# Low parts of keys and queries moved to VectorE, in a linear-attention and MLP kernel

## The chip, the core and the metric

The kernel runs on one core of a Trainium2 chip, as one program. The metric is the device time of one execution in microseconds (us), the median of several runs.

## The reference

Three layers follow each other on 4 batches of 576 tokens with 512 channels (8 heads of 64).

```python
def phi(x):                                  # x = q or k, times 64**-0.25
    h = einsum('bhsd,md->bhsm', x, omega) - sum(x*x, -1, keepdims=True)/2
    return exp(h - max(h, -1)) / sqrt(128)
kv  = einsum('bhsm,bhsd->bhmd', phi(k), v);  z = sum(phi(k), axis=2)
x   = einsum('bhsm,bhmd->bhsd', phi(q), kv) / (einsum('bhsm,bhm->bhs', phi(q), z) + 1e-6)
h   = relu(x.T @ w_tok1) @ w_tok2            # token mixing, 576 -> 256 -> 576
u   = x + h.T;   x = u + relu(u @ w_ch1) @ w_ch2           # channels, 512 -> 1536 -> 512
u   = x + real(fft(fft(x, axis=1), axis=2))
out = u + relu(layernorm(u) @ w_ff1) @ w_ff2               # 512 -> 2048 -> 512
```

The inputs of the MLP weights come as 64-bit words on the host side; the kernel turns ("widens") them into two 32-bit parts on the chip.

## The kernel before

Every matmul operand that matters for precision is split into a high part (rounded to fp32r) and a low part (the rest), and a product takes three matmuls: high by high, high by low, low by high.

**Attention.** The tokens stand in 18 tiles of 128. For each tile of keys or queries and each group g of 4 heads there is one *slot*. There are 72 slots, in this order: slots 0 to 9 are the keys of tiles k0 to k4 (two slots a tile); from slot 10 to 61 keys and queries alternate (k5 g0, q0 g0, k5 g1, q0 g1, k6 g0, ...); slots 62 to 71 are queries alone. In the loop of `attention()` the pass for slot n issues, engine by engine in program order (each engine runs its own instructions in that order):

- `load`: a tile of keys or queries is loaded by SP's queue six slots ahead of its first use (L385), with the values v (L390). The pool holds 4 such tiles, and 6 of v.
- `project`: six matmuls for slot n (L413) into a PSUM bank of tag A, of which there are four.
- `sums`: `kv_add` for the key slot n-3 (L447). A tile that holds the end of one batch and the start of the next (tiles 4 and 13) has a second, late part, one slot later.
- `queries`: for the query slot n-3, four transposes (L466) and ScalarE's copy into qpT (L474; for tiles 4 and 13 two half copies with zeros written by GpSimd beside them, L471, L472); for slot n-7 the transposed result goes to x2.
- `split_in`: four slots ahead of its first slot a tile is split. The high part is ScalarE's copy (L400; VectorE's for k1 and k3, L398), the low part t - h is one 128x512 subtraction on GpSimd (L401; on VectorE for k0 alone). Both parts are made in the same slot.
- `feature`: VectorE's maximum over each head (L427), then ScalarE's four exponentials (L431), or VectorE's subtraction and one exponential (L434, L435).
- `results`: for the query slot n-5 `numer` (L484, one PSUM pair N), and after g = 1 VectorE's `divide` (L493 to L507) and the split of the result, whose low part xl is GpSimd's (L514).
- `side.step(budget)`: a budget of VectorE time per slot for widening.
- from slot 36 on one piece of token mixing of a finished batch (L572 to L588), whose low part h1l is VectorE's (L576).

**Widening.** A chunk (4 chunks of 640 or 576 words for the token weights, then 28 slabs of 1024) is loaded (L264), worked in seven VectorE instructions (`take`, `rest`, `size`, `high`, `low`, `unit`, `scaled`: L275, L286, L290, L294, L298, L302, L306; planned at 0.68, 0.68, 0.69, 1.21, 1.21, 0.69 and 1.22 us for 1024 words, and in proportion for less) with one of ScalarE between (L282), and stored (L541 to L549, or L337). The class `Side` holds these pieces in a list, each with a planned VectorE time. A step adds its budget to a credit (at most 4.0) and issues pieces as long as the credit pays. Loads and stores cost nothing in it; a deferred one is issued four steps later. Before the change the budget is 0.7 us in slots 0 to 9, 0.4 in slots 10 to 35, and 1.2 from slot 36.

```python
            if n >= 0:
                side.step(SLOT0_US if n < 10 else SLOT1_US if n < 36 else SLOT_US)
```

By this plan, before the change, the loads of the first two chunks, and the first `take` behind them, stand in slot 0, and the store of the last token weights in slot 36.

After the attention come the two MLPs with the Fourier layer between them (L694, L816, L1129), in blocks of 512 tokens; widening goes on beside them.

Of the kernel before, what the change touches and what calls it, by code (L numbers as in the profile page):

```python
# [9 lines left out]
F32 = mybir.dt.float32  # L10
# [4 lines left out]
ALU = mybir.AluOpType  # L15
# [17 lines left out]

SLOT0_US, SLOT1_US, SLOT_US, FIRST_US, SHORT_US, CH_US, FF_US, SAVED_US = 0.7, 0.4, 1.2, 3.9, 1.2, 3.7, 3.7, 4.0


LAG, LAG_NUM, LAG_X, AHEAD_LOAD, AHEAD_SPLIT, DEFER = 3, 5, 7, 6, 4, 4
# [135 lines left out]
def pieces(t0, n):  # L175

    done = 0
    while done < n:
        b, s = divmod(t0 + done, S)
        step = min(n - done, S - s)  # L180
        yield done, step, b, s
        done += step
# [54 lines left out]
def mix_kernel(ctx: ExitStack, tc: tile.TileContext, qt, kt, va, om, w1, w2, wch, wff, t1, t2, out):  # L237
    nc = tc.nc
    pe, act, dve, pool, sync = nc.tensor, nc.scalar, nc.vector, nc.gpsimd, nc.sync
# [113 lines left out]
    def bank(tag):  # L353
        if tag not in pools:
            tag = "A"
        if tag == "A" and spare:

            tag = spare.pop(0)
            spare.append(tag)
        pl, bufs = pools[tag]  # L360
        return pl.tile([128, 512], F32, tag=tag, name=tag, bufs=bufs)
# [6 lines left out]
    e0 = p0.enter_context(tc.tile_pool(name="e0", bufs=3, side="right"))  # L368
    pl = ExitStack()
    ld = pl.enter_context(tc.tile_pool(name="ld", bufs=3))  # L370

    om_sb = e0.tile([128, 4, M], F32, tag="df", name="om_sb", bufs=2).rearrange("p a b -> p (a b)")[:, 0:256]
# [1 line left out]
    om_l = e0.tile([128, 256], F32R, name="om_l", bufs=1)  # L374

    def projection():
        sync.dma_start(out=om_sb, in_=om)
        act.mul(out=om_h, in_=om_sb, mul=scale)
        dve.scalar_tensor_tensor(out=om_l, in0=om_sb, scalar=scale, in1=om_h, op0=ALU.mult, op1=ALU.subtract)

    src = {}

    def load(kind, i):
        t = ld.tile([128, 4, 128], F32, tag="x", name=kind + "s", bufs=4)
        sync.dma_start(out=t, in_=(kt if kind == "k" else qt)[:, i])  # L385
        src[kind, i] = t
        if kind == "k":
            for part, row in enumerate([i] + [NT + c for c, j in enumerate(SPLIT) if j == i]):
                t = ld.tile([128, H, D + 1], F32, tag="v", name="v", bufs=6)
                sync.dma_start(out=t.rearrange("p h d -> p (h d)"), in_=va[row])  # L390
                src["v", i, part] = t

    def split_in(kind, i):
        t = src.pop((kind, i))
        h = ld.tile([128, 4, 128], F32R, tag="h", name=kind + "h")
        l = ld.tile([128, 4, 128], F32R, tag="l", name=kind + "l")
        if kind == "k" and i in (1, 3):
            dve.tensor_copy(out=h, in_=t)  # L398
        else:
            act.copy(out=h, in_=t)  # L400
        (dve if (kind, i) == ("k", 0) else pool).tensor_tensor(out=l, in0=t, in1=h, op=ALU.subtract)  # L401
        src[kind, i] = (h, l)

    proj = {}
    ft = {}
# [35 lines left out]
    def kv_add(i, g, part):  # L441

        off, n, b, s = part
        if s == 0:
            kvp[b, g] = bank("H")
        for hh in range(4):
            pe.matmul(out=kvp[b, g][:, hh * 65:hh * 65 + 65], lhsT=ft["k", i, g][:, hh, :],  # L447
                      rhs=src["v", i, int(off > 0)][:, 4 * g + hh, :], start=(s == 0 and hh == 0), stop=(s + n == S),
                      skip_group_check=True)
        if s + n == S:  # L450
            t = e0.tile([128, 4, D + 1], F32, tag=f"kvs{g}", name="kvs", bufs=2)
            act.copy(out=t.rearrange("p h d -> p (h d)"), in_=kvp[b, g][:, 0:260])
            kvs[b, g] = t
            if (b, g) == (B - 1, 1):
                spare.extend("AAH")
# [3 lines left out]
    num = {}  # L459
    xhl = {}  # L460

    def turn(i, g):
        tp = bank("S")
        f = ft.pop(("q", i, g))
        for hh in range(4):
            pe.transpose(tp[:, hh * 128:hh * 128 + 128], f[:, hh, :], ident)  # L466
        qpt[i, g] = []
        for off, n, b, _ in pieces(i * 128, 128):
            t = e0.tile([128, 4, 128], F32, tag="qpT", name="qpT", bufs=4)
            if n < 128:  # L470
                pool.memset(t[:, :, 64 - off:128 - off], 0.0)  # L471
                act.copy(out=t[:, :, off:off + n], in_=tp.rearrange("p (a b) -> p a b", a=4)[:, :, off:off + n])  # L472
            else:
                act.copy(out=t.rearrange("p a b -> p (a b)"), in_=tp)  # L474
            qpt[i, g].append((b, t))

# [10 lines left out]
    def divide(i):  # L487

        nm = num.pop(i)
        xt[i] = x = e0.tile([128, DM + 2], F32, tag="x", name="x", bufs=2)  # L490
        rd = e0.tile([128, 2, 4], F32, tag="rd", name="rd")
        n4 = nm[:, :, 0:260].rearrange("p g (h e) -> p g h e", e=65)
        dve.tensor_scalar(out=rd, in0=n4[:, :, :, 64], scalar1=float(M * 1e-6), scalar2=None, op0=ALU.add)  # L493
        dve.reciprocal(out=rd, in_=rd)

        def quarter(g, a, lo):
            dve.tensor_tensor(out=x[:, lo:lo + 128].rearrange("p (h e) -> p h e", e=64),  # L497
                              in0=n4[:, g, 2 * a:2 * a + 2, 0:64],
                              in1=rd[:, g, 2 * a:2 * a + 2].unsqueeze(2).to_broadcast([128, 2, 64]), op=ALU.mult)

        quarter(1, 0, 256)
        quarter(1, 1, 385)
        quarter(0, 0, 0)
        quarter(0, 1, 129)
        dve.tensor_tensor(out=x[:, 128:385:256], in0=nm[:, 1, 0:259:258], in1=rd[:, 1, 0:4:3], op=ALU.mult)  # L507
# [9 lines left out]
    def turn_x(i):  # L517
        x = xt.pop(i)
        tp = bank("S")
        for c in range(4):  # L520
            pe.transpose(tp[:, c * 128:c * 128 + 128], x[:, c * 128:c * 128 + 128], ident)
        t4 = tp.rearrange("p (c t) -> p c t", c=4)
        for off, n, b, s in pieces(i * 128, 128):
            if s == 0:
                x2[b] = xp.tile([128, 4, S], F32, tag="x2", name="x2")
            act.copy(out=x2[b][:, :, s:s + n], in_=t4[:, :, off:off + n])
# [66 lines left out]
    def last_tile(b):  # L593
        return ((b + 1) * S - 1) // 128
# [3 lines left out]
    for b in range(B):  # L598
# [3 lines left out]
        a = [("q", i, g) for i in range(qn, qe) for g in range(2)]  # L602
# [8 lines left out]
    side = Side()  # L611
# [87 lines left out]
    def attention():  # L699
        tiles = [(kind, i) for kind, i, g in order if g == 0]  # L700
        at = {t: order.index(t + (0,)) for t in tiles}
        late = {}
        n_all = len(order)

        def at_slot(n, kind):
            return order[n][1:] if 0 <= n < n_all and order[n][0] == kind else None

        def sums(n):
            if (t := at_slot(n - LAG, "k")) is not None:
                parts = list(pieces(t[0] * 128, 128))  # L710
                kv_add(*t, parts[0])
                if len(parts) > 1:
                    late[n + 1] = lambda: kv_add(*t, parts[1])
            if n in late:
                late.pop(n)()

        def queries(n):
            if (t := at_slot(n - LAG, "q")) is not None:
                turn(*t)
            t = at_slot(n - LAG_X, "q")  # L720
            if t is not None and t[1] == 1:
                turn_x(t[0])
                for b in range(B):
                    if t[0] == last_tile(b):
                        fill.extend(tok_mix(b))

        def results(n):
            if (t := at_slot(n - LAG_NUM, "q")) is not None:
                numer(*t)
                if t[1] == 1:  # L730
                    divide(t[0])
                    split_x(t[0])

        loads, splits = list(tiles), list(tiles)
        for n in range(-1, n_all + LAG_X):
            while loads and at[loads[0]] <= n + AHEAD_LOAD:
                load(*loads.pop(0))
            if n == n_all:
                enter_mlp()
            if 0 <= n < n_all:  # L740
                project(*order[n])
            sums(n)
            queries(n)
            while splits and at[splits[0]] <= n + AHEAD_SPLIT:
                split_in(*splits.pop(0))
            if 0 <= n < n_all:
                feature(*order[n])
            results(n)
            if n >= 0:
                side.step(SLOT0_US if n < 10 else SLOT1_US if n < 36 else SLOT_US)  # L750
            if fill and (len(fill) > 3 or n % 2 == 0):
                fill.pop(0)()
            for fn in early[:3]:
                fn()
            del early[:3]
# [434 lines left out]
```

## Time and profile before

| | |
|---|---|
| time, median of 3 runs | 970.43 us (970.21 to 976.52) |
| the profiled execution's own time | 972.31 us |
| its span (first to last instruction) | 970.2 us |
| PE busy | 949.7 us (98%) |
| VectorE (DVE) busy | 548.6 us (57%) |
| ScalarE (ACT) busy | 277.6 us (29%) |
| GpSimd (POOL) busy | 111.5 us (11%) |
| mean granted TensorE clock | 0.991 |

PE is TensorE's matmuls and PEld its weight loads. Matmuls overlap in the pipeline, so a PE shown as busy is not a PE at its peak: the distance from one start to the next tells its pace. Times in the rows count from the first instruction.

### The profile page before, as it was taken

How to read it: one execution, taken by the hardware profiler on the slowest of the kernel's cores; microseconds unless marked ns; L12 is line 12 of the kernel's file. 1: busy time of each engine (PE TensorE's matmuls, PEld its weight loads, DVE VectorE, ACT ScalarE, POOL GpSimd, SP SyncE). 2: the span in 40 equal slices, each digit the busy share in tenths (PEclk: the TensorE clock that was granted, in tenths of full speed). 3: DMA queues.
4: the chain of work that ended last, by engine and by line, in shares of the span. 5: the costliest groups of instructions: out<-in, count | busy, mean ns of one | idle time of the engine just before them, and what ended most of it. 6: DMA issues, size and time to landing. Idle time of an engine off the chain costs nothing.

```text
span 970.2 us, 13164 instructions
## 1 busy us (share of the span) xinstructions
PE 949.7 (98%) x5248; PEld 828.7 (85%) x5248; DVE 548.6 (57%) x1056; ACT 277.6 (29%) x621; POOL 111.5 (11%) x108
## 2 busy tenths in 40 slices
PE   7999999899999999999999999999999999999998
PEld 6999989888889988888888888888888888888897
DVE  5786988887776677766766442164346434411211
ACT  4786667642212222211311210111112111110111
POOL 2354334312110011000000000000000000000000
PEclk8899999999999999999999999999999999999999
DMA  7754554279899395364365952034103410251080
GB/s 260 241 194 161 183 184 161 104 271 334 336 351 406 126 370 207 136 251 177 116 210 208 378 174 86 1 130 174 44 1 124 162 62 1 99 205 44 16 324 30
DMA packets 33261, 170.80 MB, mean 176 GB/s; under 512 B 3632, under 2 KB 4272, under 8 KB 15664
## 3 DMA queue, kind: packets, MB, share of 16 engines
q1 hardware_dynamic: 27296, 126.91, 36.6%
q0 software_dynamic: 5904, 43.06, 11.6%
q8 instruction: 41, 0.67, 0.3%
q14 instruction: 20, 0.16, 0.1%
HBM read 132.08 MB, written 34.08 MB: 171 GB/s over the span
## 4 chain that ended last, share of the span: by engine, by line
PE 89%; DVE 7%; ACT 1%; issue 1%; DMA 1%; SPq 0%; DVEq 0%; ACTq 0%
PE H L694 35%; PE A L1129 20%; PE A L816 15%; PE A L413 3%; PE H L447 2%; PE N L484 2%; PE A L572 2%; PE S L994 1%; DVE mx L427 1%; DVE x L497 1%; PE S L1007 1%; DVE cvo L298 1%; PE S L585 1%; PE S L1113 1%; PE A L466 1%
## 5 line engine op out<-in xcount | busy, mean ns | idle before, releaser
L694 PE MATMUL H<-uh,w 128*128 128x512 f32 (+1 forms) x1120 | 341.0, 371 | 0.0
L694 PEld LDWEIGHTS H<-uh,w 128*128 128x128 f32 x1120 | 205.0, 189 | 34.9
L777 DVE SCALAR_TENSOR_TENSOR hl<-H,hh 128x512 fp32r<-128x512 f32 (+1 forms) x140 | 89.1, 637 | 256.3 <-ACT hh L776 256.1
L776 ACT ACTIVATE hh<-H 128x512 fp32r<-128x512 f32 (+1 forms) x140 | 77.8, 556 | 507.1 <-PE H L694 504.8
L694 PE MATMUL H<-ul,w 128*128 128x512 f32 (+1 forms) x560 | 206.3, 368 | 0.0
L1129 PE MATMUL A<-w,hh 128*128 128x512 f32 x576 | 146.8, 391 | 0.0
L1129 PEld LDWEIGHTS A<-w,hh 128*128 128x128 f32 x576 | 106.6, 188 | 21.0
L694 PEld LDWEIGHTS H<-ul,w 128*128 128x128 f32 x560 | 105.6, 189 | 16.8
L816 PE MATMUL A<-hh,w 128*128 128x512 f32 (+1 forms) x480 | 108.7, 369 | 0.0
L816 PEld LDWEIGHTS A<-hh,w 128*128 128x128 f32 x480 | 84.2, 188 | 15.0
L1129 PE MATMUL A<-w,hl 128*128 128x512 f32 x288 | 80.6, 390 | 0.0
L1129 PEld LDWEIGHTS A<-w,hl 128*128 128x128 f32 x288 | 54.1, 188 | 11.4
L431 ACT ACTIVATE f<-A,mx 128x128 f32<-128x128 f32 x204 | 58.9, 382 | 14.1 <-DVE mx L427 13.8
L816 PE MATMUL A<-hl,w 128*128 128x512 f32 (+1 forms) x240 | 59.2, 368 | 0.0
L427 DVE TENSOR_REDUCE mx<-A 128x4 f32<-128x512 f32 x71 | 48.4, 682 | 11.4 <-PE A L413 9.8
L816 PEld LDWEIGHTS A<-hl,w 128*128 128x128 f32 x240 | 42.6, 188 | 7.6
L447 PE MATMUL H<-v,f 128*128 128x65 f32 x320 | 44.4, 287 | 1.9 <-ACT f L431 1.3
L447 PEld LDWEIGHTS H<-v,f 128*128 128x128 f32 x320 | 43.2, 209 | 2.6 <-ACT f L431 1.8
L484 PE MATMUL N<-kvs,qpT 128*128 128x65 f32 x320 | 40.1, 270 | 3.0 <-DVE x L507 3.0
L484 PEld LDWEIGHTS N<-kvs,qpT 128*128 128x128 f32 x320 | 38.9, 193 | 3.7 <-POOL ql L401 2.4
L306 DVE SCALAR_TENSOR_TENSOR cvo<-cvo,cvy 128x1024 fp32r<-128x1024 f32 (+2 forms) x32 | 40.0, 1248 | 0.0
L294 DVE SCALAR_TENSOR_TENSOR cvo<-cvy,cvo 128x1024 int32<-128x1024 int32 (+2 forms) x32 | 38.9, 1215 | 0.5
(185 smaller groups left out, 1183.2 us busy)
## 6 DMA issues: line engine op xcount, KB each, us to landing
w<-kept SPq DMA_DIRECT2D x80, 1024.0 KB, 5.1
kept<-cvo POOLq DMA_DIRECT2D x21, 1024.0 KB, 6.8
stg<-in_wff_dram POOLq DMA_DIRECT2D x16, 1024.0 KB, 6.3
stg<-in_wch_dram SPq DMA_DIRECT2D x9, 1024.0 KB, 4.8
kept<-cvo SPq DMA_DIRECT2D x7, 1024.0 KB, 4.6
v<-in_va_dram SPq DMA_DIRECT2D x20, 260.0 KB, 3.8
ks<-in_kt_dram SPq DMA_DIRECT2D x18, 256.0 KB, 3.7
qs<-in_qt_dram SPq DMA_DIRECT2D x18, 256.0 KB, 4.0
```

The lines of the kernel that those rows point to most:

```text
L294: dve.scalar_tensor_tensor(out=st["h"], in0=st["y"].bitcast(I32), scalar=-0x80000000, in1=st["h"], op0=ALU.bitwise_and, op1=ALU.bitwise_or)
L306: dve.scalar_tensor_tensor(out=st["o"][:, 1, 0:n], in0=st["l"].bitcast(F32), scalar=2.0 ** -52, in1=st["y"], op0=ALU.mult, op1=ALU.mult)
L413: pe.matmul(out=pj[:, p_ * 256:p_ * 256 + 256], lhsT=a[:, c, :], rhs=w, start=(n == 0), stop=(n == 2), skip_group_check=True)
L427: dve.tensor_reduce(out=mx, in_=p4, axis=AX.X, op=ALU.max, negate=True)
L431: act.activation(out=f[:, hh], in_=p4[:, hh], func=AF.Exp, bias=mx[:, hh])
L447: pe.matmul(out=kvp[b, g][:, hh * 65:hh * 65 + 65], lhsT=ft["k", i, g][:, hh, :], rhs=src["v", i, int(off > 0)][:, 4 * g + hh, :], start=( ...
L484: pe.matmul(out=nm[:, hh * 65:hh * 65 + 65], lhsT=t[:, hh, :], rhs=kvs[b, g][:, hh, :], start=(c == 0), stop=(c == len(ts) - 1), skip_grou ...
L694: pe.matmul(out=hb[:, 0:n], lhsT=a[:, kk * 128:kk * 128 + 128], rhs=u[:, kk, 0:n], start=(c == 0), stop=(c == 11))
L776: act.activation(out=hh, in_=hb[:, 0:n], func=AF.Relu)
L777: dve.scalar_tensor_tensor(out=hl, in0=hb[:, 0:n], scalar=0.0, in1=hh, op0=ALU.max, op1=ALU.subtract)
L816: pe.matmul(out=acc[i][:, 0:cols], lhsT=a[:, cs], rhs=v, start=(j == 0 and c_ == 0), stop=(j == NCH - 1 and c_ == 2))
L1129: pe.matmul(out=acc[t], lhsT=a[:, t * 128:t * 128 + 128], rhs=w, start=(j == 0 and c_ == 0), stop=(j == NFF - 1 and c_ == 2))
```

## The change

- The low part of each tile of keys and queries goes from GpSimd to VectorE, and is issued one slot after the high part, ahead of that slot's splits and maximum (k0's at once, as before).
- Widening: no step before slot 2, steps with a budget of zero in slots 2 to 5 (they issue the first loads alone), 1.2 us in slots 6 to 9, 0.45 in 10 to 35, 1.2 from 36. By the planner the first `take` comes in slot 6, and the store of the last token weights in slot 38.
- The late part of `kv_add` comes two slots after the first instead of one, and first in its slot.
- The zeros beside half tiles of queries are written once, at the start, into one tile for each g.
- omega is loaded on ScalarE's queue instead of SP's.
- Three tiles of keys and queries in the pool instead of four, three whole qpT instead of four, two rd instead of three.

```diff
-SLOT0_US, SLOT1_US, SLOT_US, ... = 0.7, 0.4, 1.2, ...
+SLOT0_US, SLOT1_US, SLOT_US, ... = 1.2, 0.45, 1.2, ...
...
-        sync.dma_start(out=om_sb, in_=om)
+        act.dma_start(out=om_sb, in_=om)
...
-        t = ld.tile([128, 4, 128], F32, tag="x", name=kind + "s", bufs=4)
+        t = ld.tile([128, 4, 128], F32, tag="x", name=kind + "s", bufs=3)
...
+    rest = []
...
-        (dve if (kind, i) == ("k", 0) else pool).tensor_tensor(out=l, in0=t, in1=h, op=ALU.subtract)
         src[kind, i] = (h, l)
+        rest.append(lambda: dve.tensor_tensor(out=l, in0=t, in1=h, op=ALU.subtract))
+        if (kind, i) == ("k", 0):
+            rest.pop()()
...
+    mixed_q = [e0.tile([128, 4, 192], F32, name=f"mq{g}", bufs=1) for g in range(2)]
+    for t in mixed_q:
+        pool.memset(t[:, :, 64:128], 0.0)
...
-            t = e0.tile([128, 4, 128], F32, tag="qpT", name="qpT", bufs=4)
             if n < 128:
-                pool.memset(t[:, :, 64 - off:128 - off], 0.0)
-                act.copy(out=t[:, :, off:off + n], in_=tp.rearrange("p (a b) -> p a b", a=4)[:, :, off:off + n])
+                act.copy(out=mixed_q[g][:, :, 2 * off:2 * off + n],
+                         in_=tp.rearrange("p (a b) -> p a b", a=4)[:, :, off:off + n])
+                t = mixed_q[g][:, :, off:off + 128]
             else:
+                t = e0.tile([128, 4, 128], F32, tag="qpT", name="qpT", bufs=3)
...
         def sums(n):
+            if n in late:
+                late.pop(n)()
...
-                    late[n + 1] = lambda: kv_add(*t, parts[1])
-            if n in late:
-                late.pop(n)()
+                    late[n + 2] = lambda: kv_add(*t, parts[1])
...
             queries(n)
+            while rest:
+                rest.pop(0)()
             while splits and at[splits[0]] <= n + AHEAD_SPLIT:
                 split_in(*splits.pop(0))
...
-            if n >= 0:
-                side.step(SLOT0_US if n < 10 else SLOT1_US if n < 36 else SLOT_US)
+            if n >= 2:
+                side.step(0.0 if n < 6 else SLOT0_US if n < 10 else SLOT1_US if n < 36 else SLOT_US)
```

## Rows read from the trace of the kernel before

**Rows 1.** The page: the chain that ended last, share of the span by engine.

```profile
PE 89%; DVE 7%; ACT 1%; issue 1%; DMA 1%; SPq 0%; DVEq 0%; ACTq 0%
```

**Rows 2.** Windows over the attention: stretch, length, busy time of each engine, clock.

```profile
12.22:33.40 21.18, 19.81 (x115) 19.41 (x114) 16.66 (x26) 13.60 (x40) 6.39 (x5) 0.68 0.80 250
33.40:76.29 42.89, 42.11 (x369) 41.73 (x368) 35.39 (x71) 37.56 (x104) 20.96 (x17) 1.00 0.62 204
76.29:165.17 88.88, 84.96 (x660) 80.92 (x660) 73.52 (x137) 58.86 (x152) 33.16 (x24) 1.00 0.48 162
165.17:190.24 25.07, 21.53 (x171) 20.91 (x170) 21.75 (x46) 17.41 (x42) 9.42 (x11) 0.93 0.40 156
```

**Rows 3.** Window of the low clock.

```profile
18.98:32.60 13.62, 13.62 (x67) 13.62 (x67) 10.79 (x16) 9.39 (x27) 5.13 (x4) 0.51 0.82 245
```

**Rows 4.** Timeline to 18 us: start, length, engine, line, work, [idle before it].

```profile
0.74 0.38 SPq L377 DMA_DIRECT2D om_sb<-in_om_dram  x1
1.19 0.42 SPq L385 DMA_DIRECT2D ks<-in_kt_dram  x1
...
4.02 0.43 SPq L385 DMA_DIRECT2D ks<-in_kt_dram  x1
...
4.85 0.62 ACT L400 CAST kh<-ks 128x512 fp32r<-128x512 f32 x1 [1.59 <-DMA ks<-in_kt_dram]
...
5.50 0.69 DVE L401 TENSOR_TENSOR kl<-ks,kh 128x512 fp32r<-128x512 f32 x1 [1.78 <-ACT kh L400]
...
11.21 0.49 DVE L275 TENSOR_SCALAR cvy<-stg 128x640 f32<-128x640 f32 x1 [2.28 <-DMA stg<-in_w_dram]
11.62 0.69 DVE L427 TENSOR_REDUCE mx<-A 128x4 f32<-128x512 f32 x1
...
16.02 1.21 PE L447 MATMUL H<-v,f 128*128 128x65 f32 x8 [1.26 <-ACT f L431]
```

**Rows 5.** DMA issues to 12 us: count, size, median us from issue to landing.

```profile
ks<-in_kt_dram SPq DMA_DIRECT2D x6, 256.0 KB, 4.6
```

**Rows 6.** Timeline: starts of projections at either clock, and of slot 12's maximum.

```profile
22.50 0.56 PE L413 MATMUL A<-om_h,kh 128*128 128x256 f32 x1
...
25.49 0.56 PE L413 MATMUL A<-om_h,kh 128*128 128x256 f32 x1
...
34.44 0.69 DVE L427 TENSOR_REDUCE mx<-A 128x4 f32<-128x512 f32 x1 [0.52 <-ACT kvs L452]
...
41.12 0.36 PE L413 MATMUL A<-om_h,kh 128*128 128x256 f32 x1
...
44.75 0.36 PE L413 MATMUL A<-om_h,kh 128*128 128x256 f32 x1
```

**Rows 7.** Groups of one line and form, attention: count, busy us, mean ns, idle before.

```profile
L427 DVE TENSOR_REDUCE mx<-A 128x4 f32<-128x512 f32 x71 | 48.4, 682 | 11.4 <-PE A L413 9.8 <-ACT qpT L474 1.0 <-ACT kvs L452 0.5
...
L298 DVE SCALAR_TENSOR_TENSOR cvo<-cvo,stg 128x1024 f32<-128x1024 int32 x8 | 11.2, 1399 | 0.0
...
L286 DVE TENSOR_SCALAR cvo<-stg 128x1024 int32<-128x1024 int32 x8 | 6.1, 760 | 0.0
L576 DVE SCALAR_TENSOR_TENSOR h1l<-A,h1h 128x512 fp32r<-128x512 f32 x6 | 4.2, 692 | 12.0 <-ACT h1h L575 12.0
```

**Rows 8.** The same view of GpSimd.

```profile
L401 POOL TENSOR_TENSOR ql<-qs,qh 128x512 fp32r<-128x512 f32 x18 | 28.8, 1598 | 23.2 <-ACT qh L400 19.3 <-PE H L447 4.0
L514 POOL TENSOR_TENSOR xl<-x,xh 128x512 fp32r<-128x512 f32 x18 | 26.7, 1483 | 37.2 <-ACT xh L513 32.5 <-issue 4.2 <-PE A L413 0.4
L401 POOL TENSOR_TENSOR kl<-ks,kh 128x512 fp32r<-128x512 f32 x17 | 22.0, 1292 | 78.2 <-ACT kh L400 67.2 <-DVE kh L398 11.0
```

**Rows 9.** Timeline: the late stretch, and VectorE beside GpSimd's xl.

```profile
180.76 2.15 PE L484 MATMUL N<-kvs,qpT 128*128 128x65 f32 x16 [2.19 <-DVE x L507]
...
218.27 1.29 POOL L514 TENSOR_TENSOR xl<-x,xh 128x512 fp32r<-128x512 f32 x1 [4.21 <-issue]
...
218.36 2.28 DVE L306 SCALAR_TENSOR_TENSOR cvo<-cvo,cvy 128x1024 fp32r<-128x1024 f32 x1
```

More of the change, by code (lines that the diff above doesn't have):

```diff
@@ L32 @@
 BLOCKS = [0, NBLK - 1, *range(1, NBLK - 1)]
-SLOT0_US, SLOT1_US, SLOT_US, FIRST_US, SHORT_US, CH_US, FF_US, SAVED_US = 0.7, 0.4, 1.2, 3.9, 1.2, 3.7, 3.7, 4.0
+SLOT0_US, SLOT1_US, SLOT_US, FIRST_US, SHORT_US, CH_US, FF_US, SAVED_US = 1.2, 0.45, 1.2, 3.9, 1.2, 3.7, 3.7, 4.0
 LAG, LAG_NUM, LAG_X, AHEAD_LOAD, AHEAD_SPLIT, DEFER = 3, 5, 7, 6, 4, 4
@@ L490, in divide @@
         xt[i] = x = e0.tile([128, DM + 2], F32, tag="x", name="x", bufs=2)
-        rd = e0.tile([128, 2, 4], F32, tag="rd", name="rd")
+        rd = e0.tile([128, 2, 4], F32, tag="rd", name="rd", bufs=2)
         n4 = nm[:, :, 0:260].rearrange("p g (h e) -> p g h e", e=65)
```

## The prediction

> **What bounds the kernel now.** I read the chain that ended last first: 89% of it is PE, 7% VectorE [rows 1]. Only what shortens or delays PE's own sequence can move the end. The change touches the attention, the first 220 us; behind it PE works without a gap worth naming, so the end should move by what the attention's end moves. The windows by stage come next [rows 2]. There the reader sees two things. From 33 us on PE is nearly full (42.1 of 42.9 us, then 85.0 of 88.9) while VectorE is at 83% and stays there (35.4 of 42.9, 73.5 of 88.9, 21.8 of 25.1). In 12 to 33 us PE looks full as well (19.8 of 21.2), but the clock column says 0.68: it is slow, not loaded. The window of the low clock puts it at 18.98 to 32.60 us at 0.51, that is 1.2 instead of 2.4 GHz, with PE busy in all of it [rows 3].
>
> The timeline of the start shows why. VectorE's first widening instruction stands in its queue ahead of slot 1's maximum, and waits 2.28 us for its DMA, to 11.21 us; that maximum starts at 11.62. The delay runs on through ScalarE's exponentials until PE sits 1.26 us before the sum at 16.02 [rows 4], 3 us before the clock falls. A key slot at the low clock takes 25.49 - 22.50 = 2.99 us; two slots at the full one, a key and a query, take 44.75 - 41.12 = 3.63 [rows 6].
>
> **Part by part: the start.** omega leaves SP's queue, where its issue took the first 0.45 us (0.74 to 1.19) [rows 4]; k0's load is issued that much earlier, and so is k0's high part at 4.85, behind which PE starts. Gain 0 to 0.45 us, I take 0.4. ScalarE issues omega's load in about the same 0.4 us ahead of its table load, and still waits for it.
>
> k3's load, issued at 4.02 without a wait, must now wait for the low part of k0 (three tiles in the pool), which ends at 5.50 + 0.69 = 6.19 [rows 4]. With 4.6 us to landing [rows 5] and the shift of 0.4 it is there at about 10.4. VectorE's copy of k3 stands ahead of slot 2's maximum and waits for it, some 0.8 us in which nothing else is late, as PE is still in the projections of the first tiles.
>
> Without widening VectorE has in slots 2 to 5 a maximum (0.68 each) [rows 7], two low parts and one difference, under 1.4 us a slot; PE needs about 1.6 for a key slot at full clock (an estimate: half of the 3.63 less some 0.4 for the query's transposes). So PE should run through without the gap of 16.02. Placed by hand: slot 4 at 11.9, then 1.5 us a slot, slot 12 at about 24, if the clock stays up.
>
> But VectorE then sets the pace. Between the high part of k4 and slot 12's maximum it has seven maxima, two differences and five low parts, 14 instructions at 0.69 alone (k0's row [rows 4]) and, as I estimate, 0.6 where one overlaps the next: 8.4 to 9.7 us. Widening adds 4 x 1.2 + 3 x 0.45 = 6.2 by the budgets, of which the planner has issued 5.3. That is 13.7 to 15.0 us from 14.3 on, the time I estimate for k4's high part behind ScalarE's exponentials. Slot 12's maximum comes at 28.0 to 29.3 instead of 34.44 [rows 6]. I take 28.0, as VectorE has a queue there and waits for nobody: 6.4 us earlier. If PE's own 24 counted, against its 33.4 [rows 2], it would be 9.4.
>
> **The low parts.** 35 leave GpSimd (18 of queries, 17 of keys, 28.8 + 22.0 = 50.8 us there [rows 8]) and come to VectorE at 0.69 each: 24.3 us. Something comes back. VectorE's widening is slower beside GpSimd: `low` takes 1.40 on average against the planned 1.21. Over the seven groups of 1024 words (57 instructions, from L298 to L286) the excess is 9.0 us [rows 7]; with the same per instruction for the 28 smaller ones 13.4. L401 has 50.8 of the 77.5 us of GpSimd's three groups [rows 8], so 8.8 us of it goes away. Between 0 and 13.4; I take 8.8.
>
> What a low part costs when it meets GpSimd's xl has no row: no subtraction of this kind stood beside one. Nearest is the `scaled` piece that ran with an xl and took 2.28 [rows 9] instead of 1.22, 1.06 more. Some 14 xl fall in these slots: 0 to 15 us; VectorE's order puts the low parts a slot before most divides, so I take one in four, 3.5 us.
>
> The Trainium skill (SBUF — State Buffer, "Who interferes with whom") says that a VectorE instruction with two SBUF inputs contends with a GpSimd instruction that reads SBUF. The row of 2.28 agrees with that rule. By it alone, with every xl meeting a low part, the 3.5 would be 15: that is part of rival 3 below.
>
> So VectorE gets 24.3 - 8.8 + 3.5 = 19 us of work more. I divide it by stretch: the low parts by their slots (7 before slot 12, then 11, 14 and 3), what comes back by GpSimd's busy time (6.4, 21.0, 33.2, 9.4 [rows 2]). What of it lies on the path?
>
> Slots 12 to 33 (33.4 to 76.3 before): 11 x 0.69 - 2.6 + 1.2 for xl and 1.0 for the larger budget, 7.2 more. VectorE comes to 35.4 + 7.2 = 42.6 of 42.9 us, PE has 42.1 [rows 2]. Both fit, neither with room, and VectorE enters with PE 4 us ahead of it, so that PE's waits are covered at first. Between -1.5 and +4; I take 0.5 lost.
>
> 76 to 165 us: 14 x 0.69 - 4.2 + 1.6 = 7.1 more, beside 15 us of idle time [rows 2]. Much of that is VectorE standing before ScalarE's h1h, 12.0 us in six places [rows 7], behind PE's longest runs, and is not to be had. A quarter on the path, 1.8, between 0 and 5.
>
> 165 to 190 us: VectorE is the one that is late. It is busy 21.8 of 25.1 us [rows 2], and PE waits 2.19 us for a divide [rows 9]. Three low parts come in: 2.1 - 1.2 + 0.5 = 1.4, of which I take 1.2.
>
> **The rest.** The late part of `kv_add` two slots later removes at most the wait of 0.52 us at slot 12's kvs copy [rows 6] and its like; half a microsecond. The zero writes of GpSimd stand in 4 of the 36 query slots, behind its low parts; no wait of PE's that I saw ends with one, so zero. The pool of three is worth nothing later: a load still comes four slots before the split. The store of the last token weights comes in slot 38 instead of 36, and its first reader also stands in slot 38, behind two runs of 15 long matmuls in slots 36 and 37; these cover it. Without that cover PE would wait up to the 4.6 us of a landing [rows 5].
>
> **Sum.** The 0.4 is contained in the 6.4. Thus -6.4 + 0.5 + 1.8 + 1.2 - 0.5 = -3.4 us. On the profiled execution's 972.3 (its span of 970.2 and 2.1 around it) that gives 968.9. The median of the runs is 1.9 below that execution, and I forecast the median: 967.0.
>
> **Rivals.** (1) *VectorE keeps up.* The contention that goes away is worth more than I take, and the late stretch is not worse: only the 6.4 and more arrive, to PE's own limit of 9.4. 961 to 963.5, say 962.5. For it: in 33 to 76 us both engines fit. Against it: the divide at 180 us is late already. (2) *The clock falls again.* Slots 6 to 9 give VectorE 2.4 us each for PE's 1.6. If the lead of three slots is used up by slot 9 or 10, PE pauses as it did at 16.02, and the low clock lasts 13.6 us as before, half of it lost: 6.8. The -3.4 becomes +3.4: 974. It decides once PE pauses in slots 8 to 13 for as long as that 1.26 [rows 4]. For it: a single gap of 1.26 went ahead of the fall. Against it: that fall came behind several late maxima, here there is a lead. (3) *VectorE binds to the end of the attention.* All 15.7 us from slot 12 on come onto the path, or low parts meet an xl each time and add 11 on VectorE: -6.4 + 15.7 - 0.5 = +8.8, 979. Against it stand the 12 us for h1h, which can't all be lost again. (4) *The start doesn't move.* The maxima come earlier but the clock falls just the same, a DMA or the v tiles taking over as what is late: the gain is 0.4 to 2, given back later; 970.
>
> **How the numbers follow.** The forecast has 0.45 (964 to 970), (1) 0.20, (2) 0.17, (3) 0.07, (4) 0.11. The range leaves out the outer ends of (1), and (3): 961 to 975. One per cent, 9.7 us, is about what a measurement of this kernel can tell from no change. Faster by that asks for under 960.7, the far end of (1): 0.06. Slower asks for over 980.1, past (3): 0.03. The rest, 0.91.
>
> **What would show it.** Slot 12's maximum near 28 us and no window at 0.5 between 15 and 30 us; if it is there, rival 2 or 4. VectorE's `size` at 0.68 wherever no xl stands beside it. Low parts at 0.69, some above 1. In the windows, VectorE over 90% in 33 to 70 us with PE still at over 95%. PE's wait for the divide in the last query slots longer than 2.2 us; if it has gone, rival 1. The prediction is wrong if ScalarE's high parts come late and VectorE's queue stands behind them, which the trace before cannot show.

## The result and the profile after

The changed kernel takes 977.36 us, median of 11 runs (973.23 to 978.21), against 970.43 for the kernel before, median of nine (968.39 to 976.62). By the means of these runs it takes 1.0052 times as long, interval 1.0032 to 1.0072. The forecast was 967.0, in a range of 961 to 975, so both the sign and the range were missed. (Runs of before at 981 us and more, with a mean granted clock of 0.981 or less, are left out of every comparison; with them the median of its 11 runs is 970.83.) The profiled execution has a span of 976.0 us, 5.8 more than before.

The page of after, busy time by engine and the chain that ended last:

```profile
PE 948.2 (97%) x5248; PEld 826.7 (85%) x5248; DVE 563.6 (58%) x1091; ACT 278.3 (29%) x621; POOL 57.9 (6%) x67
...
PE 89%; DVE 7%; ACT 2%; DMA 1%; issue 1%; DVEq 0%; ACTq 0%
```

The shares are those of [rows 1]: a chain that is 89% PE doesn't tell where 6 us were lost. Reading by slots does. The stretches below run from the start of one slot's projection to that of another (the table has before and after, and the experiments that follow; the stretches are those of the one execution that was profiled, the ratio is that of the means of all runs):

| kernel | slots 0-16 | 16-33 | 33-61 | 61-71 | slot 71 at | span | median | ratio [95%] |
|---|---|---|---|---|---|---|---|---|
| before | 35.60 | 35.17 | 87.37 | 32.56 | 196.22 | 970.2 | 970.43 | |
| after | 32.93 | 35.32 | 93.28 | 34.34 | 201.19 | 976.0 | 977.36 | 1.0052 [1.0032, 1.0072] |
| after_lows_gpsimd | 28.79 | 35.01 | 86.76 | 33.13 | 189.00 | 963.3 | 967.97 | 0.9977 [0.9955, 0.9999] |
| before_lows_vector | 36.99 | 35.29 | 95.80 | 34.61 | 207.77 | 982.5 | 987.01 | 1.0171 [1.0126, 1.0216] |
| before_begin_later | 35.71 | 35.27 | 87.47 | 33.32 | 196.85 | 971.2 | 969.94 | 0.9996 [0.9974, 1.0018] |
| after_budget_even | 27.69 | 36.16 | 92.80 | 34.53 | 196.46 | 971.2 | 970.83 | 1.0005 [0.9983, 1.0026] |
| after_late_lows_gpsimd | 29.89 | 35.49 | 86.84 | 34.76 | 192.26 | 966.6 | 969.23 | 0.9992 [0.9976, 1.0009] |
| after_lows_behind_max | 34.35 | 35.61 | 87.40 | 36.42 | 199.00 | 974.0 | 975.89 | 1.0038 [1.0007, 1.0068] |
| lows_gpsimd_reduce_vector | 35.58 | 36.22 | 93.56 | 36.62 | 207.38 | 982.1 | 982.96 | 1.0108 [1.0065, 1.0151] |
| after_scale_early | 27.58 | 40.04 | 91.61 | 34.00 | 198.54 | 973.4 | 971.76 | 1.0001 [0.9977, 1.0025] |
| behind_even | 31.38 | 36.70 | 87.95 | 35.33 | 196.60 | 971.4 | 972.84 | 1.0032 [1.0009, 1.0055] |
| gpsimd_even | 27.26 | 35.23 | 87.71 | 33.56 | 189.07 | 963.9 | 966.85 | 0.9967 [0.9950, 0.9984] |
| gpsimd_late1 | 34.32 | 34.79 | 87.51 | 31.52 | 193.58 | 967.9 | 971.02 | 1.0002 [0.9981, 1.0022] |
| before_begin_even | 26.55 | 34.88 | 88.78 | 33.80 | 188.59 | 963.5 | 964.93 | 0.9945 [0.9924, 0.9966] |

From before to after: -2.7 us up to slot 16, nothing to slot 33, +5.9 to slot 61, +1.8 to slot 71. Windows of after: slots 0 to 4, 4 to 12, 12 to 33, 33 to 61, on to 195.18 us, and the low clock; columns as in [rows 2]:

```profile
5.32:11.28 5.96, 5.96 (x32) 5.74 (x33) 5.41 (x10) 2.46 (x7) 0.00 (x0) 1.00 0.94 300
11.28:25.54 14.26, 13.42 (x115) 13.02 (x114) 11.18 (x19) 9.07 (x26) 0.00 (x0) 1.00 0.66 235
25.54:73.57 48.03, 45.72 (x368) 45.10 (x368) 43.22 (x90) 40.52 (x115) 5.88 (x4) 0.93 0.68 207
73.57:166.85 93.28, 84.90 (x646) 81.03 (x646) 80.61 (x151) 58.75 (x148) 10.73 (x7) 0.98 0.47 166
166.85:195.18 28.33, 23.39 (x185) 22.55 (x183) 25.45 (x53) 18.81 (x47) 3.28 (x3) 0.94 0.41 158
30.40:37.20 6.80, 6.80 (x35) 6.80 (x34) 4.49 (x7) 3.46 (x11) 0.00 (x0) 0.50 1.04 295
```

Three things are to be seen. Up to 25.54 us the clock column holds 1.00 where it was 0.68 before [rows 2]. Then it falls after all, for 6.8 us at 0.50, half as long as in [rows 3]. And from 73.57 on VectorE is busy 80.6 of 93.3 us, while PE stands idle 93.28 - 84.90 = 8.4 us, against 87.37 - 83.45 = 3.9 in the same slots of before. That window of before, and PE's longest waits in it (waiting, what for, us in total, times, longest):

```profile
76.29:163.66 87.37, 83.45 (x646) 79.41 (x646) 72.01 (x134) 57.35 (x148) 32.26 (x23) 1.00 0.48 161
...
PE A L521 <- ACT f L431: 1.2, 1, 1.2
PE A L572 <- ACT f L431: 1.1, 1, 1.1
```

All of PE's waits in the window of after:

```profile
PE A L533 <- DVE cvy L275: 3.5, 2, 1.8
PE A L597 <- ACT f L436: 3.5, 3, 1.4
PE A L584 <- ACT f L436: 1.0, 2, 0.5
PE A L533 <- DVE x L600: 0.3, 1, 0.3
```

These are 8.3 us. Line 436 (L431 before) is the exponentials, which empty PSUM banks. The two waits that stand under `take` (L275) are theirs as well: `take` empties no bank, and an exponential had ended 0.02 us ahead of it each time (99.73 and 99.75, 151.39 and 151.41). So PE waits 8.0 us for exponentials where before it waited 2.3. The timeline shows one such chain:

```profile
108.80 1.50 POOL L526 TENSOR_TENSOR xl<-x,xh 128x512 fp32r<-128x512 f32 x1 [11.40 <-ACT xh L525]
...
109.43 1.42 DVE L405 TENSOR_TENSOR kl<-ks,kh 128x512 fp32r<-128x512 f32 x1
...
110.77 0.68 DVE L432 TENSOR_REDUCE mx<-A 128x4 f32<-128x512 f32 x1
...
111.48 1.14 ACT L436 ACTIVATE f<-A,mx 128x128 f32<-128x128 f32 x4 [1.24 <-DVE mx L432]
...
112.67 0.53 PE L597 MATMUL A<-w2hl,h1h 128*128 128x288 f32 x2 [1.29 <-ACT f L436]
```

A low part stands ahead of the maximum on VectorE and beside an xl, and takes 1.42 us instead of 0.69. The maximum and the exponentials start that much later, ScalarE has waited 1.24 us, and PE 1.29. Before, the low part was GpSimd's, and the maximum didn't have it in front.

VectorE's groups of after in the attention (columns as in [rows 7]):

```profile
L432 DVE TENSOR_REDUCE mx<-A 128x4 f32<-128x512 f32 x71 | 48.4, 683 | 2.0 <-PE A L418 1.7
...
L405 DVE TENSOR_TENSOR kl<-ks,kh 128x512 fp32r<-128x512 f32 x18 | 14.6, 809 | 3.3 <-ACT kh L403 3.2
...
L405 DVE TENSOR_TENSOR ql<-qs,qh 128x512 fp32r<-128x512 f32 x18 | 13.5, 750 | 0.7 <-ACT qh L403 0.7
...
L298 DVE SCALAR_TENSOR_TENSOR cvo<-cvo,stg 128x1024 f32<-128x1024 int32 x8 | 10.4, 1304 | 0.0
...
L588 DVE SCALAR_TENSOR_TENSOR h1l<-A,h1h 128x512 fp32r<-128x512 f32 x6 | 4.2, 692 | 11.9 <-ACT h1h L587 11.9
```

The maxima no longer wait for PE (1.7 us in all, 9.8 before [rows 7]): VectorE comes late to nearly every one. The 11.9 us ahead of h1l stayed, as the forecast had it.

### The profile page after: what moved, and what is told of

Same layout as the page of the kernel before. It is cut to its first block, busy times and chain, and to the rows that moved or that the text cites. A ratio compares the mean times of both kernels' runs of the same rounds, so it can differ in the third digit from the quotient of the medians.

```text
span 976.0 us, 13150 instructions
## 1 busy us (share of the span) xinstructions
PE 948.2 (97%) x5248; PEld 826.7 (85%) x5248; DVE 563.6 (58%) x1091; ACT 278.3 (29%) x621; POOL 57.9 (6%) x67
## 3 DMA queue, kind: packets, MB, share of 16 engines
q0 software_dynamic: 5904, 43.06, 11.6%
## 4 chain that ended last, share of the span: by engine, by line
PE 89%; DVE 7%; ACT 2%; DMA 1%; issue 1%; DVEq 0%; ACTq 0%
PE H L706 35%; PE A L1144 20%; PE A L831 15%; PE A L418 3%; PE N L496 2%; PE H L452 2%; PE A L584 2%; PE S L1009 1%; DVE mx L432 1%; ACT f L436 1%; DVE x L509 1%; PE S L1022 1%; PE S L597 1%; PE S L1128 1%; DVE kl L405 1%; PE A L597 1%
## 5 line engine op out<-in xcount | busy, mean ns | idle before, releaser
L1144 PE MATMUL A<-w,hl 128*128 128x512 f32 x288 | 80.6, 390 | 0.0
L1144 PEld LDWEIGHTS A<-w,hl 128*128 128x128 f32 x288 | 54.1, 188 | 11.4
L526 POOL TENSOR_TENSOR xl<-x,xh 128x512 fp32r<-128x512 f32 x18 | 27.0, 1498 | 196.4 <-ACT xh L525 196.4
L298 DVE SCALAR_TENSOR_TENSOR cvo<-cvo,stg 128x1024 f32<-128x1024 int32 (+2 forms) x32 | 37.9, 1185 | 0.0
```

The lines of the kernel that those rows point to most:

```text
L298: dve.scalar_tensor_tensor(out=st["l"].bitcast(F32), in0=st["l"], scalar=2.0 ** 32, in1=st["lw"].bitcast(U32), op0=ALU.mult, op1=ALU.add)
L1144: pe.matmul(out=acc[t], lhsT=a[:, t * 128:t * 128 + 128], rhs=w, start=(j == 0 and c_ == 0), stop=(j == NFF - 1 and c_ == 2))
```

## The clock of each run: a second way to read the times

Every run comes with the mean granted clock of its execution, and the executions of one kernel differ in it. Before takes 967.0 us at 0.996, 970.6 at 0.993 and 974.7 at 0.988: about 1.0 us for each thousandth. So times at one clock can be compared, to about half a microsecond, as the clock is given to a thousandth; what is left is not the clock (medians, number of runs in brackets):

| kernel | 0.998 | 0.996 | 0.993 |
|---|---|---|---|
| before | | 967.0 (8) | 970.6 (15) |
| after | 973.6 (2) | | 977.5 (7) |
| after_lows_gpsimd | 965.1 (4) | 966.9 (2) | 970.1 (4) |
| before_begin_later | 967.5 (4) | | 972.3 (2) |
| after_late_lows_gpsimd | | 968.2 (5) | 971.1 (2) |
| after_lows_behind_max | | | 975.9 (10) |
| lows_gpsimd_reduce_vector | | | 981.4 (3) |
| after_budget_even | 969.7 (3) | 970.7 (5) | |
| gpsimd_even | 965.4 (3) | 967.2 (6) | |
| behind_even | | 971.1 (4) | |
| after_scale_early | 970.3 (2) | 971.7 (5) | |
| gpsimd_late1 | | | 971.0 (3) |
| before_begin_even | 964.8 (5) | 965.6 (1) | |

At 0.993 after is 6.9 us slower than before, and after_lows_gpsimd, which differs from after only in who makes the low parts, is within 0.5 us of before. So the low parts on VectorE are the whole loss, and the rest of the change is worth something only where it holds the clock up.

## Experiments

Of the theories, the first says that it is VectorE's added work, from slot 33 on, that sets the time, wherever it stands in its slot; the second, that it is the place of the low parts ahead of the maximum; the start, with its budgets, is judged beside them.

**The low parts back on GpSimd.** All else as in after.

```diff
-        rest.append(lambda: dve.tensor_tensor(out=l, in0=t, in1=h, op=ALU.subtract))
+            rest.append(lambda: pool.tensor_tensor(out=l, in0=t, in1=h, op=ALU.subtract))
```

> The changed kernel with one thing undone: the 35 low parts are GpSimd's again, still one slot behind the high ones. Theory 1 (VectorE's added work is on the path from slot 33 on, and its lag in slots 6 to 12 makes PE pause and the clock fall): the 7.7 us that slots 36 to 71 lost against the kernel before come back, and the lag at slot 13 shrinks by five low parts of 0.69, so the clock may hold as well: 969 if it falls all the same, 963 if it holds. Rival (the later place of the low parts, the late sums or the pool of three cost the time, whoever computes them): stays at 976 to 978.

967.97 us (964.98 to 971.82), 9.4 below after; slots 33 to 61 fall from 93.28 to 86.76. The window of that stretch:

```profile
69.11:155.87 86.76, 83.36 (x647) 79.47 (x646) 75.88 (x136) 57.55 (x146) 35.72 (x22) 1.00 0.54 178
```

VectorE has 4.7 us less to do there and the stretch is 6.5 shorter, 1.5 of it less PE time (83.36 against 84.90), as the clock column is 1.00 and not 0.98. At equal clock the low parts cost 7.4 (0.993) to 8.4 us (0.998).

**The low parts alone.** Before with its low parts on VectorE, one slot behind, and no other part of the change.

```diff
+        rest.append(lambda: dve.tensor_tensor(out=l, in0=t, in1=h, op=ALU.subtract))
...
+            while rest:
+                rest.pop(0)()
             while splits and at[splits[0]] <= n + AHEAD_SPLIT:
```

> The kernel before with the low parts on VectorE one slot behind, and nothing else of the change. Theory 1: slots 33 to 71 lose 7 to 8 us as in the changed kernel, and the start isn't gained: 977 to 980. Rival (the low parts are covered by idle time of VectorE and by the faster widening beside an idle GpSimd, the loss comes from other parts): 970 to 972.

987.01 us, 16.6 slower than before and past the 977 to 980. Its one run at 0.991 took 979.8, where before takes 971.6 (3 runs), and its one run at 0.988 took 984.2 against 974.7: 8.2 to 9.5 is the low parts' own, the rest lies in the clock. Four stretches of low clock stand in the attention in its trace, the first of them 13.7 us long, from 19.6 us on.

**The later widening alone.** Before with the budgets of after and nothing in slots 0 to 5.

```diff
-            if n >= 0:
-                side.step(SLOT0_US if n < 10 else SLOT1_US if n < 36 else SLOT_US)
+            if n >= 2:
+                side.step(0.0 if n < 6 else SLOT0_US if n < 10 else SLOT1_US if n < 36 else SLOT_US)
```

> The kernel before with the new budgets of widening alone (no step before slot 2, zero to slot 5, 1.2 in slots 6 to 9, 0.45 in 10 to 35). Theory 1: the start is gained (the trace of the changed kernel shows slot 11 9.0 us earlier) and little is given back, as VectorE has no low parts: 961 to 965. Rival (the heavy slots 6 to 9 alone make PE pause and the clock fall): 968 to 971, with a window of the low clock between 25 and 40 us.

969.94 us (965.82 to 973.23): no difference, so the rival came true. The low clock comes from about 27 us on instead of 19, and lasts 13.7 us again. PE waits 1.46 us for exponentials at 24.59, ahead of it, and 1.61 for a kvs copy at 29.72, in it. Its runs lie at a higher clock than those of before, but at equal clock it is 1.4 to 1.7 us slower (970.0 against 968.6 at 0.995, 972.3 against 970.6 at 0.993).

**The budget spread evenly.** After with 0.7 us in slots 6 to 9 and 0.53 from 10 to 35, the same sum.

```diff
-SLOT0_US, SLOT1_US, ... = 1.2, 0.45, ...
+SLOT0_US, SLOT1_US, ... = 0.7, 0.53, ...
```

> The changed kernel with the widening after slot 6 spread evenly: 0.7 us in slots 6 to 9 and 0.53 in 10 to 35 instead of 1.2 and 0.45, the same sum within 0.4 us. Theory 1: VectorE is 2 us less behind at slot 10, ScalarE's kvs copy comes in time, PE doesn't pause before slot 13 and the clock holds until slot 36: 970 to 972. Rival (the clock falls at that place whatever VectorE's lag, by the key slots' own light load on PE): 976 to 978 with a window of the low clock before 40 us.

970.83 us (969.45 to 973.02), 6.5 below after. Slots 0 to 16 take 27.69 instead of 32.93, with no low clock ahead of 97 us; PE's pause ahead of the late sum is 0.36. Slots 33 to 61 stay at 92.80. At 0.998 it is still 3.9 us faster than after: the rest of its gain is not the clock.

**Only the later half on GpSimd.** The low parts of k0 to k10 and q0 to q5 stay on VectorE (17), the other 19 go back.

```diff
+        eng = pool if i >= (11 if kind == "k" else 6) else dve
+        rest.append(lambda: eng.tensor_tensor(out=l, in0=t, in1=h, op=ALU.subtract))
```

> The changed kernel with the 19 low parts whose slot is 31 or later (k11 to k17, q6 to q17) given back to GpSimd; the 16 earlier ones stay on VectorE. Theory 1 (VectorE's added work costs from slot 33 on, and the clock falls early from the lag of slots 6 to 12, two separate losses): slots 33 to 61 take 87 to 88 us again instead of 93.3, the early clock fall stays: 969 to 971. Rival (the late loss is a consequence of the early lag or of the later place): 976 to 978.

969.23 us (966.32 to 971.39). Slots 33 to 61 take 86.84. At 0.993 it is 1.0 us above after_lows_gpsimd and 6.4 below after: the early half, 557.4 - 550.1 = 7.3 us of VectorE's time, costs 1 us; the later one, 563.6 - 557.4 = 6.2 us, costs all of its own length. It isn't that VectorE had time to spare in the first half: with these low parts it is busy 38.3 of the 40 us from 30 to 70.

**The low parts behind the maximum.** The same instructions on the same engine, one place later in each slot.

```diff
-            while rest:
-                rest.pop(0)()
+            ready = list(rest)
+            rest.clear()
...
                 feature(*order[n])
+            for fn in ready:
+                fn()
```

> The changed kernel with each low part issued behind its slot's maximum instead of ahead of it; the work on VectorE is the same. If the loss is by the place (each maximum comes 0.7 us and a wait for ScalarE's high part later, ScalarE and PE behind it): slots 33 to 61 fall from 93.3 to 88 to 90 and the time to 970 to 973. If it is the sum of VectorE's work (theory 1): within 1.5 us of the changed kernel, 976 to 978.

975.89 us (973.75 to 979.81), not the gain that the second theory gave. Its windows of slots 33 to 61 and 61 to 71:

```profile
75.18:162.58 87.40, 83.27 (x646) 79.47 (x646) 77.82 (x150) 57.35 (x146) 10.06 (x7) 1.00 0.51 177
162.58:199.00 36.42, 31.16 (x221) 29.57 (x220) 31.26 (x65) 22.52 (x56) 5.09 (x4) 0.91 0.34 129
```

The stretch that after lost in is whole again, but the next one is 2.1 us longer, and slots 0 to 16 1.4. In the start PE now waits for a low part itself (1.29 us at 25.39). At 0.993 only 1.6 of the 7.4 us are won. The place decides in which stretch the cost appears, and little of how much it is.

**Other work of the same length in the same place.** The low parts on GpSimd; VectorE takes a maximum over each tile in their place, which is overwritten (work that nothing needs).

```diff
+                dve.tensor_reduce(out=l[:, :, 0:1], in_=t, axis=AX.X, op=ALU.max)
+                pool.tensor_tensor(out=l, in0=t, in1=h, op=ALU.subtract)
```

> The changed kernel with the low parts on GpSimd, and on VectorE in the place of each a maximum of the same tile of 128x512 (0.68 us, one input, no wait for the high part), whose result is overwritten by the low part. So VectorE is as occupied as in the changed kernel, but waits for no high part and reads one input. Occupation alone (theory 1): slots 33 to 61 take 92 to 95 us as in the changed kernel, and more, as widening is slowed by GpSimd too: 976 to 981. If what costs is the wait for ScalarE or the meeting with xl: 88 us or less there, and 966 to 970.

982.96 us (981.25 to 984.08), past the 976 to 981, slots 33 to 61 93.56. The added instruction takes 0.67 us, reads one tile, and doesn't wait for ScalarE's high part, and the time is lost all the same. So neither that wait nor the meeting of a low part with an xl is needed for the loss in slots 33 to 61, where PE waits 6.2 us for exponentials and 1.8 for VectorE, and never for GpSimd. In the start it has a wait that after has not, 2.58 us for a low part of GpSimd, which stands behind the added maximum; ahead of slot 33 the run is thus no clean test. With GpSimd working as before nothing is won back by VectorE's other instructions: it is busy 575.7 us, 25.6 more than in after_lows_gpsimd, and the time at 0.993 is 11.4 longer.

**The scaling without its lag.** In after, ScalarE's step of each widening piece (line 282) is issued one planner step after VectorE's first; here right behind it.

```diff
-            side.later(scale, 1)
+            scale()
```

> The changed kernel with ScalarE's instruction of widening issued with the take instead of a step later, which removes the 1.9 us in which VectorE stood before the first size behind ScalarE's exponentials in slot 7. If that stall is what the lead of slots 6 to 12 was lost by: PE's pause before slot 13 (1.43 us) shrinks to under 0.5 and the clock holds until slot 36: 970 to 972. If the pause comes from the low parts and the budget of 1.2 in any case: 976 to 978, slot 13 no more than 2 us earlier.

971.76 us (970.11 to 975.13), 5.6 below after, 3.3 of it at equal clock (0.998). Slots 0 to 16 take 27.58. The clock doesn't hold until slot 36: PE pauses 1.04 us for exponentials at 42.62, the clock falls at about 45 us for 6.8 us, and 16 to 33 takes 40.04.

**Both behind the maximum and even; GpSimd and even.** The edits of above with 0.7 and 0.53.

> The changed kernel with both suspected costs cured and all 35 low parts still on VectorE: each low part behind its slot's maximum, and widening at 0.7 us in slots 6 to 9 and 0.53 in 10 to 35. Theory 2 (in slots 33 to 61 the place of the low part ahead of the maximum costs some 6 us, not VectorE's sum of work; the early fall of the clock is a second loss of some 6): slots 33 to 61 at 87 to 89 us, no low clock before 100 us: 965 to 968. Rival (the sum of the work comes out somewhere else, or the better stretch of the earlier run was chance): 970 to 973.

> The changed kernel with the low parts on GpSimd and the even budget (0.7 in slots 6 to 9, 0.53 in 10 to 35). Theory 2: nothing ahead of the maximum, VectorE less behind in slots 6 to 12, PE's pause of 1.4 us for ScalarE's kvs copy before slot 13 gone, the clock up from slot 4 to 36 in every run: 963 to 966, the fastest of all. Rival (the low clock isn't set by that pause): 967 to 969 as with the budget of 1.2.

972.84 us (970.52 to 978.72) and 966.85 (963.97 to 970.38). At 0.996 the first is 3.9 us above the second, and after_budget_even 3.5: with even budgets the place of the low parts makes no difference to the sum. The 965 to 968 that the second theory gave for low parts behind the maximum isn't reached, and that theory falls as an account of the whole; nor does the clock hold there, as PE waits 1.63 us for a low part at 25.98 and the clock is low for 3.4 us from 26.3 on.

**Late parts one slot later, as before.** after_lows_gpsimd with `late[n + 1]`, issued at the end of the slot's sums.

> The changed kernel with the low parts on GpSimd and the late part of a sum one slot behind the first again, at the end of its slot. If the late part's place is of no weight: 967 to 969, as with two slots. If it is what kept PE from pausing in slots 12 to 13 (the kernel before with the later widening alone paused there and its clock fell): the low clock stands between 26 and 40 us and the time is 970 to 973.

971.02 us (968.89 to 972.95), 3.1 above after_lows_gpsimd, 1.0 of it at equal clock (0.993). PE waits 2.19 us for a kvs copy, up to 29.07, and within that wait, at 28.6, a low clock of 10.2 us begins.

**The best of it.** Before with the later widening and the even budget, nothing else.

> The kernel before with widening begun later and evenly (no step before slot 2, zero to slot 5, 0.7 in slots 6 to 9, 0.53 in 10 to 35), and nothing else of the change. Theory 2: VectorE is no longer behind at slot 12, PE runs through and the clock holds, as the low parts are on GpSimd: 962 to 966, slot 16 near 33 us. If the later beginning alone doesn't carry it (late parts, pool or omega's queue are needed): 968 to 971 as with the budget of 1.2.

964.93 us (963.91 to 965.59), ratio 0.9945, interval 0.9924 to 0.9966: faster than both kernels. Its windows of the first two stretches:

```profile
4.58:31.13 26.55, 26.13 (x212) 25.77 (x213) 21.49 (x33) 19.43 (x58) 10.65 (x9) 1.00 0.82 287
31.13:66.01 34.88, 34.34 (x300) 33.99 (x300) 31.75 (x67) 32.06 (x92) 20.41 (x16) 1.00 0.78 237
```

PE is busy 26.13 of 26.55 us at a clock of 1.00. Slot 16 starts 10.0 us earlier than before (31.13 against 41.12 [rows 6]; 0.9 of it because k0's load, issued at the same time, landed earlier in this execution). At slot 71 7.6 us are left, and 5.5 in the medians (970.39 before beside it). Five of its six runs have a mean clock of 0.998.

## Why the prediction was wrong

**Right: the mechanism of the start.** Without a widening instruction that waits for its DMA in front of the maxima, PE runs through slots 4 to 11 at the full clock. Slot 4 was placed at 11.9 and starts at 11.28, k4's high part at 14.3 and its low part starts at 14.09, slot 12 at 24 and it starts at 25.54. That is worth the clock: before_begin_even, which is this part alone with an even budget, gains 5.5 us (964.93 against 970.39), where 6.4 was forecast. With the budgets of the change itself the same part gained nothing (before_begin_later, 969.94).

The forecast was a gain of 3.4 us, and the profiled execution lost 5.8. Of these 9.2 us 3.7 lie in the start (6.4 forecast, 2.7 gained at slot 16) and 4.1 in slots 33 to 61 (1.8 forecast, 5.9 lost). Two steps failed.

**Wrong: "VectorE has a queue there and waits for nobody".** Slot 12's maximum was to come at 28.0 us; it comes at 30.76, 3.7 earlier than before and not 6.4. From the timeline of after:

```profile
14.09 0.69 DVE L405 TENSOR_TENSOR kl<-ks,kh 128x512 fp32r<-128x512 f32 x1 [1.06 <-ACT kh L403]
...
20.66 0.76 ACT L282 ACTIVATE cvy<-cvy 128x640 f32<-128x640 f32 x1
...
21.45 0.49 DVE L290 TENSOR_SCALAR cvo<-cvy 128x640 int32<-128x640 int32 x1 [1.90 <-ACT cvy L282]
...
28.58 0.75 ACT L282 ACTIVATE cvy<-cvy 128x640 f32<-128x640 f32 x1
29.21 0.39 ACT L457 COPY kvs<-H 128x260 f32<-128x260 f32 x1
...
29.65 2.16 PE L452 MATMUL H<-v,f 128*128 128x65 f32 x12 [1.43 <-ACT kvs L457]
...
30.76 0.68 DVE L432 TENSOR_REDUCE mx<-A 128x4 f32<-128x512 f32 x1
```

The work was counted rightly: from 14.09 to 30.76 VectorE is busy 14.1 us, where 13.7 was forecast. The waits were put at nothing, and they are the rest. The 1.06 us for k4's high part lie within the forecast's 14.3; the 1.90 for the scaling do not. The scaling stands in ScalarE's queue behind exponentials. Those wait for maxima, and the maxima for VectorE: two queues that each work in order and wait for each other. The same scaling stands ahead of the kvs copy at 28.58, and PE pauses 1.43 us for that copy. Then the clock falls (30.40). after_scale_early, which takes the lag of the scaling out, has slot 12's maximum at 28.60, close to the 28.0, and 27.58 in slots 0 to 16 instead of 32.93; after_budget_even has 28.71 and 27.69. These two show what made the maximum late; what makes the clock fall stays open (below).

**That was rival 2,** with its condition (a pause as long as 1.26 in slots 8 to 13; here it comes behind slot 13's projection) and a smaller price: 6.8 us at half the clock, 3.4 lost, where half of 13.6 was put down. Its chance of 0.17 was too small: I let the lead of PE stand against it, and the lead was gone at slot 13.

**Wrong: how much of VectorE's work lies on the path.** The work itself was nearly right: 15.0 us more (563.6 against 548.6) where 19 was forecast. Against 0.69 each the low parts were stretched by 14.6 + 13.5 - 36 x 0.69 = 3.3 us (3.5 estimated). But the step "a quarter on the path" for slots 33 to 61, 1.8 us, failed: it was 5.9, some 1.5 of it a stretch of low clock that before hasn't there. The terms for slots 12 to 33 (0.5; 0.15 measured from slot 16 on) and for the last stretch (1.2; 1.8) were about right; in the last one PE waits up to 3.0 us for a divide (2.19 before [rows 9]). In all I put 3.5 of 19 us on the path, 0.18 for each us. The runs show more, at equal clock, from VectorE's busy time in the profiles and the table above:

| pair | VectorE, us | time, us | per us |
|---|---|---|---|
| before_lows_vector - before | 17.3 | 8.2 to 9.5 | 0.47 to 0.55 |
| after - after_lows_gpsimd | 13.5 | 7.4 to 8.4 | 0.55 to 0.62 |
| after_lows_behind_max - after_lows_gpsimd | 11.6 | 5.8 | 0.50 |
| lows_gpsimd_reduce_vector - after_lows_gpsimd | 25.6 | 11.4 | 0.44 |
| after_budget_even - gpsimd_even | 9.6 | 3.5 to 4.3 | 0.36 to 0.45 |
| behind_even - gpsimd_even | 9.3 | 3.9 | 0.42 |

So it is the first theory that holds for the sum, whatever the place in the slot: about half of each added us comes out at the end. The reason that I gave for a small share was the 12.0 us in which VectorE stands before h1l. They stay idle (11.9 in after), but I misread where they lie: [rows 7] covers the whole attention, and only four of the six places, 8.6 us, are in 76 to 165 us; the other two come at 197 and 202. In 76 to 165 VectorE was idle 15.4 us, 6.8 of them elsewhere, and 7.1 us of work were to come in. I should have read it as the second bound there. The run with only the later half on GpSimd shows where the price is paid: 0.14 per us in the first half, 1.0 in the later one. What makes the halves differ, with VectorE at 83% in both before, no run shows. Rival 3 was the nearest to this: of its 15.7 us half came, 7.9 from slot 16 to 71.

**Small terms.** omega off SP's queue was to bring 0.4 us; PE starts at 5.32 instead of 5.52, as omega now lands 3.6 us after its issue (2.1 before) and ScalarE waits 1.88 us for it. The late parts two slots later were put at 0.5; they are worth 1.0 at equal clock and 3.1 with it. What came back from contention is larger than 8.8: 35 low parts take 28.1 - 0.7 = 27.4 us, VectorE grew by 15.0, so 12.4 came back; `low` (L298), for one, went from 1399 to 1304 ns on average. The Trainium skill (SBUF — State Buffer, "Who interferes with whom") names contention of a VectorE instruction with two SBUF inputs and a GpSimd one that reads SBUF. The rows agree with it: the low part of 1.42 us above stood beside an xl.

**Open.** What decides the early fall of the clock. In after_lows_gpsimd PE pauses as long, for the same copy, and its profiled execution holds the clock:

```profile
28.71 0.55 PE L453 MATMUL H<-v,f 128*128 128x65 f32 x3 [1.42 <-ACT kvs L458]
```

Four of its runs lie at 0.998 (965.1 us) and four at 0.993 (970.1), so the same kernel goes either way; only profiles of several of its executions could tell what is different between them. The zeros and the pool of three were not tried alone; at equal clock, all parts but the low parts come to -0.2 to -0.5 us together. Late parts two slots later on top of before_begin_even weren't tried either.

## What to carry to other kernels

Where an engine is busy for over 80% of a stretch beside a full PE, take its idle time apart by what ends it and by where it lies: here most of it was one wait that couldn't be used, and added work went on the path at about half its length, though both engines would have fitted. The share alone doesn't tell: at the same 83% added work cost 0.14 of its length in the first half and all of it in the later one. Before you give an engine work that another did off the path, ask what it takes from the engine's in-order partners: here ScalarE and VectorE waited for each other, and the late one stopped PE. Give a planner's budget evenly: bunched in four slots the same sum cost 6.5 us in after, 5.0 in the kernel before, and 1.1 with the low parts on GpSimd.

## What the runs showed of the hardware

Of the 14 profiles nine show the clock fall from 2.4 to 1.2 GHz between 18 and 50 us, for 3.4 to 13.7 us. In each of the nine PE had paused for 1.0 to 2.6 us shortly before (in gpsimd_late1 the fall came within the pause), and it is busy in all of the 6.8 us of after. Three profiles without a pause of over 0.5 us up to 50 us (after_budget_even, gpsimd_even, before_begin_even) show no fall there. Two with a pause of 1.42 us (after_lows_gpsimd, after_late_lows_gpsimd) show none either: the pause went with every early fall, but didn't always bring one. Executions of one kernel differ by 2 to 10 us, and most of that goes with the mean granted clock, 1.0 us for each thousandth. Sorted by their clock the runs give 3.5 to 9.5 us for the low parts, where the medians gave 4.0, 9.4 and 16.6.
